# Routing rebuilt and traced first; two score blocks of the next quarter moved into the old one

## Chip, cores and metric

The kernel runs on one core of a Trainium2 chip. The metric is device time in microseconds, the median of several executions. TensorE (PE in the profile) multiplies matrices, VectorE (DVE), ScalarE (ACT) and GpSimd (POOL) work on elements, SyncE (SP) issues most transfers. SBUF is the on-chip memory, PSUM the accumulators that TensorE writes, in banks of 512 fp32 columns.

## Reference

Three parts, one after the other: an attention with random exponential features over 4 batches, 8 heads, 576 positions; a mixture of 8 experts in which each token takes the expert of its largest logit; and a dense network.

```python
q_p, k_p = (phi(q_s), phi(k_s))          # phi: exp(x @ omega.T - |x|^2/2 - row maximum)
kv = np.einsum('bhsm,bhsd->bhmd', k_p, v)
...
num = np.einsum('bhsm,bhmd->bhsd', q_p, kv)
den = np.einsum('bhsm,bhm->bhs', q_p, z)[..., None] + 1e-06
...
logits = x @ w_gate
expert_idx = np.argmax(logits, axis=1)
probs = np.exp(logits_shift)
probs /= probs.sum(-1, keepdims=True) + 1e-09
...
    h = np.maximum(xe @ w1[e], 0.0)
    ye = h @ w2[e]
    out[mask] = gate_w[mask, None] * ye
...
h = x @ w_in
g = h * (1.0 / (1.0 + np.exp(-1.702 * h)))
return (g @ w_out).astype(np.float32)
```

## The kernel before

The attention is worked in eight quarters, each half of a batch's heads (four heads). For each quarter `qgen` handles the queries and `kgen` the keys. `ph_P` is a score block: TensorE multiplies transposed queries or keys with omega into a PSUM tile `pr`, VectorE takes the row maximum (L359) into a slot of the one-bank PSUM tile `small`, two small operations (L368) combine it with half the squared norm, and a subtraction (L380) writes `qp` or `kp`. `X` transposes `qp` on TensorE and ScalarE takes the exponent into `qpT`; `N` multiplies it with `kv` and VectorE normalises (L446 to L455) into `xn`; `XT` (the R steps) transposes `xn` into the tile `tx` and, for the last 64 positions, into columns 0 to 63 of `small`, from where ScalarE writes the high part `xh` and VectorE the low part `xl`. `Q_ORDER` lists the order of these steps in a quarter; it has 17.

`route(b)` follows when both quarters of batch b are done. It multiplies `xh` and `xl` with the gate weights (`lT_ps`, two halves), copies the 16 rows (high and low part of the weights) to `lT`, transposes them, adds the halves, marks each token's largest logit (`oh`), counts the tokens of each expert with a product against ones (`ct_ps`), takes the index of the largest count (`ci`, `es`) and reads it into a register of SyncE. The expert weights w1[e], w2[e] of the batch are then requested in eight pieces by `pump` and `stage` (`st`), split into `wh` and `wl`, and multiplied by `moe_gen` (`m_ps`): the kernel works the expert that most tokens of a batch take, and tokens of another expert are handled by a loop at the end that is entered only if there are any. The products of a batch can't begin before its routing; batch 0's routing runs in the third quarter.

The order in which work is written down ("traced") is made by generators: `merge` always calls the part with the smallest share of its weight done (query steps weight 17, routing `ROUTE_N`, keys 5), and an outer loop alternates attention and experts by summed costs. A scheduler then orders each engine's queue, with earlier traced work first where it expects it to be ready. Each engine, and SyncE's transfer queue, works its queue in order.

```python
parts = [(qgen(i), W_Q)]
if pending is not None:
    parts.append((route(pending), ROUTE_N))
```

## Time and profile before

| | us |
|---|---|
| median of 3 runs | 767.72 (767.65 to 769.79) |
| the profiled execution | 767.65 |
| its span, first to last instruction | 765.6 |
| TensorE busy | 739.7 |
| VectorE busy | 531.3 |
| ScalarE busy | 338.6 |
| GpSimd busy | 131.9 |

The span is what the profile's rows add up to; the profiled execution's own time is 2.05 us longer and is what the prediction is made against. Busy shares are averages over stages with different limits, so the stages are read by themselves.

### The profile page before, as it was taken

What the parts mean: (1) busy time and instruction counts of PE and PEld (TensorE: products, weight loads), DVE (VectorE), ACT (ScalarE), POOL (GpSimd) and SP (SyncE); (2) the same over time, 40 slices, a digit from 0 to 9 for tenths busy, and PEclk for the clock granted to TensorE, in tenths of its full rate; (3) what the DMA queues carried; (4) which work ended last, traced back from release to release, by engine and by line L of the source; (5) the groups of instructions that cost most, each with busy time, mean ns of one, the idle gap of its engine ahead of it and who ended that gap; (6) DMA issues with size and microseconds to landing.
All of it is one profiled execution on the core that took longest, in us unless ns stands there. A gap on an engine that the chain in (4) does not pass through costs nothing.

```text
span 765.6 us, 14359 instructions
## 1 busy us (share of the span) xinstructions
PE 739.7 (97%) x5559; PEld 716.1 (94%) x5559; DVE 531.3 (69%) x1188; ACT 338.6 (44%) x638; POOL 131.9 (17%) x78
## 2 busy tenths in 40 slices
PE   7998799999999999989999999999999999999997
PEld 6877699999999999979999999999999999999996
DVE  5867867586776685556879559981368777777774
ACT  5554464335522332233427464554576433444331
POOL 3563377609500441000000000000000000000000
PEclk9999799999999999999999999999999999999999
DMA  5447594456725554198145558972978544443311
GB/s 157 117 131 187 123 302 97 120 140 193 189 60 162 150 179 134 51 234 287 59 161 197 177 171 295 316 263 100 332 273 298 172 138 138 137 129 117 115 29 32
DMA packets 136715, 127.57 MB, mean 167 GB/s; under 512 B 58176, under 2 KB 120896, under 8 KB 135744
## 3 DMA queue, kind: packets, MB, share of 16 engines
q1 hardware_dynamic: 123936, 98.85, 43.5%
q10 hardware_dynamic: 12704, 27.73, 10.3%
q8 instruction: 45, 0.74, 0.4%
q14 instruction: 30, 0.25, 0.1%
HBM read 79.68 MB, written 40.40 MB: 157 GB/s over the span
## 4 chain that ended last, share of the span: by engine, by line
PE 83%; DVE 8%; DMA 4%; issue 1%; ACT 1%; SPq 1%; POOL 0%; ACTq 0%; POOLq 0%; DVEq 0%
PE m_ps L136 19%; PE qa L1249 13%; PE qa L1146 13%; PE qm L1249 7%; PE w_ps L136 4%; PE pb L1249 3%; PE qm L1146 3%; PE qu L1146 3%; PE num L444 3%; PE kv_ps L402 3%; DMA st<-in_moe_w_dram 2%; PE qn L1146 2%; PE qt L1146 2%; PE tq L430 1%; PE pr L344 1%
## 5 line engine op out<-in xcount | busy, mean ns | idle before, releaser
L1146 PE MATMUL qa<-y,wi 128*128 128x384 f32 x576 | 109.2, 337 | 0.4 <-DVE g L901 0.4
L1146 PEld LDWEIGHTS qa<-y,wi 128*128 128x128 f32 x576 | 101.4, 188 | 0.8 <-DVE g L901 0.8
L136 PE MATMUL m_ps<-xh,wh 128*128 128x288 f32 x256 | 79.0, 309 | 4.1 <-DVE h1l L735 2.3
L136 PE MATMUL m_ps<-xh,wl 128*128 128x288 f32 x256 | 76.8, 300 | 0.1
L136 PE MATMUL m_ps<-xl,wh 128*128 128x288 f32 x256 | 76.4, 298 | 0.0
L700 POOL TENSOR_TENSOR wl<-st,wh 128x1024 fp32r<-128x1024 f32 x23 | 55.1, 2401 | 83.0 <-ACT wh L698 82.9
L359 DVE TENSOR_REDUCE small<-pr 128x4 f32<-128x512 f32 (+1 forms) x80 | 51.1, 639 | 11.8 <-PE pr L351 7.8
L698 ACT ACTIVATE wh<-st 128x1024 fp32r<-128x1024 f32 (+1 forms) x33 | 34.0, 1035 | 48.5 <-DMA st<-in_moe_w_dram 31.6
L136 PEld LDWEIGHTS m_ps<-xh,wh 128*128 128x128 f32 x256 | 48.6, 190 | 5.8 <-DVE h1l L735 3.6
L136 PE MATMUL m_ps<-h1h,wh 128*128 128x288 f32 x160 | 48.8, 305 | 0.9 <-DVE h1l L735 0.9
L136 PEld LDWEIGHTS m_ps<-xh,wl 128*128 128x128 f32 x256 | 48.6, 190 | 0.5 <-DVE wl L700 0.4
L735 DVE SCALAR_TENSOR_TENSOR h1l<-m_ps,h1h 128x288 fp32r<-128x288 f32 x64 | 28.9, 453 | 28.9 <-ACT h1h L732 28.8
L136 PEld LDWEIGHTS m_ps<-xl,wh 128*128 128x128 f32 x256 | 48.6, 190 | 0.0
L136 PE MATMUL m_ps<-h1l,wh 128*128 128x288 f32 x160 | 47.7, 298 | 0.0
L136 PE MATMUL m_ps<-h1h,wl 128*128 128x288 f32 x160 | 47.4, 298 | 0.0
L732 ACT ACTIVATE h1h<-m_ps 128x288 fp32r<-128x288 f32 x64 | 25.9, 407 | 48.5 <-PE m_ps L136 46.7
L1249 PE MATMUL qa<-p,p 128*128 128x256 f32 x360 | 46.2, 282 | 1.1 <-DVE p L855 0.8
L1249 PE MATMUL qa<-p,gs 128*128 128x256 f32 x360 | 45.9, 282 | 0.0
L1249 PEld LDWEIGHTS qa<-p,p 128*128 128x128 f32 x360 | 44.2, 189 | 1.6 <-DVE p L855 1.0
L1249 PEld LDWEIGHTS qa<-p,gs 128*128 128x128 f32 x360 | 44.2, 189 | 0.0
L444 PEld LDWEIGHTS num<-kv,qpT 128*128 128x128 f32 (+1 forms) x320 | 36.7, 184 | 5.4 <-ACT qpT L432 3.1
L444 PE MATMUL num<-kv,qpT 128*128 128x65 f32 (+1 forms) x320 | 39.3, 266 | 2.5 <-ACT qpT L432 1.4
(213 smaller groups left out, 1819.5 us busy)
## 6 DMA issues: line engine op xcount, KB each, us to landing
g_dram<-g ACTq DMA_DIRECT2D x48, 384.0 KB, 4.1
st<-in_moe_w_dram SPq DMA_DIRECT2D x31, 512.0 KB, 5.2
pg<-g_dram SPq DMA_DIRECT2D x10, 1024.0 KB, 5.7
raw<-in_moe_w_in_dram SPq DMA_DIRECT2D x16, 512.0 KB, 4.0
gt<-g_dram SPq DMA_DIRECT2D x8, 1024.0 KB, 5.4
p<-wo_dram SPq DMA_DIRECT2D x6, 1024.0 KB, 7.3
yt<-y_dram SPq DMA_DIRECT2D x12, 384.0 KB, 6.0
vm<-in_v_dram SPq DMA_DIRECT2D x32, 128.0 KB, 3.2
```

The costliest lines, as they stand in the source:

```text
L136: ins = nc.tensor.matmul(out=ps, lhsT=a, rhs=b, start=start and n == 0, stop=stop and n == 2)
L344: nc.tensor.matmul(out=ps[:, :, h2], lhsT=xT[:, (2 * pr + h2) * 2 + t0 // 2], rhs=wbd)
L359: nc.vector.tensor_reduce(out=pm, in_=ps[:, :w], axis=AX.X, op=ALU.max, negate=on_act)
L402: nc.tensor.matmul(out=kv_ps[:, h, :], lhsT=kp[j // 2][:, j % 2, h2, :], rhs=vm[:, h, t, :], start=(t == 0), stop=False,)
L430: nc.tensor.transpose(tq[:, c, h2], qp[i][:, c, h2, :], ident)
L444: nc.tensor.matmul(out=ps[:n, c, h2, :], lhsT=lhsT, rhs=kv[:, h, :])
L698: nc.scalar.activation(out=hi[:, :, s], in_=st[:, :, s], func=ACTF.Copy)
L700: eng.tensor_tensor(out=lo[:, :, s], in0=st[:, :, s], in1=f32(hi)[:, :, s], op=ALU.subtract)
L732: nc.scalar.activation(out=hh[:, f], in_=ps, func=ACTF.Relu)
L735: nc.vector.scalar_tensor_tensor(out=hl[:, f], in0=ps, scalar=0.0, in1=f32(hh[:, f]), op0=ALU.max, op1=ALU.subtract)
L1146: ins = nc.tensor.matmul(out=ps, lhsT=w[:, a, ks], rhs=y[:, b, kk], start=start and kk + m == 0, stop=kk == 1 and m == 2, skip_group_check ...
L1249: ins = nc.tensor.matmul(out=ps, lhsT=x[:, f], rhs=w[i][:, f], start=start and f + m == 0, stop=f == NP - 1 and m == 2, skip_group_check=True,
```

## The change

Routing gets the weight 40 in `merge`, in every quarter that has one. The logits' transposition becomes a product with a 16 by 8 matrix `fold` that adds the halves, into columns 256 to 295 of `small`; the counts go to columns 384 to 423 of `small`, with a product of their own for the last 64 positions in place of a cleared one-hot. The expert's number is read, and the weights requested, before exponent and gate are computed; the per-token index is made from the one-hot and `left` (8 minus the expert's number) instead of five searches for maximum and index. `F0` and `F1` in `Q_ORDER` compute score blocks 0 and 1 of the next quarter, which skips them.

```diff
--- before.py
+++ after.py
@@ -62,7 +62,7 @@
     XQ = nc.sync
     DVE_LO = 1
     KPRE = 6
-    ROUTE_N = 10
+    ROUTE_N = 40
     HP_ROUTE = 0
     HP_SPLIT = (0, 3)
     HP_STAGE = (0,)
@@ -72,7 +72,7 @@
     W_Q = 17
     W_K = 5
     K_ORDER = (0, 1, 4, 2, 3)
-    Q_ORDER = "P0 P1 X0 P4 X1 N0 P2 X4 N1 X2 P3 N4 X3 N2 R0 N3 R1"
+    Q_ORDER = "P0 P1 X0 P4 X1 N0 P2 X4 N1 X2 P3 N4 X3 N2 F0 R0 N3 F1 R1"
     LAG_E = 2
     LAG_X = 1
     LAG_M = 0
@@ -183,6 +183,7 @@
     QB = H // QH
     NQ = B * QB
     asked = []
+    first = {}
     clock = [0]
     late = []
 
@@ -420,7 +421,7 @@
         src, kv = q_in.pop(i), kv_t.pop(i)
         xn = att.tile([P, T + 1, QH, D], F32, tag="xn", name="xn", bufs=1)
         xv = xn.rearrange("p t h d -> p t (h d)")
-        qp, qt = {}, {}
+        qp, qt = first.pop(i, {}), {}
 
         def X(i):
             w = 2 if i < 4 else 1
@@ -485,7 +486,9 @@
                 xh_t[b] = (moe if b % 2 else xep).tile([P, KD, S], F32R, tag="xh", name="xh", bufs=1)
                 xl_t[b] = (moe if b % 2 else xep).tile([P, KD, S], F32R, tag="xl", name="xl", bufs=1)
             if op[0] == "P":
-                c = ph_P(i, src, qp, "qp", 3, g)
+                c = 0 if g in qp else ph_P(i, src, qp, "qp", 3, g)
+            elif op[0] == "F":
+                c = ph_P(i + 1, q_in[i + 1], first.setdefault(i + 1, {}), "qp", 3, g) if i + 1 < NQ else 0
             else:
                 c = {"X": X, "N": N, "R": XT}[op[0]](g)
             if n == 0 and i + 1 < NQ:
@@ -507,6 +510,12 @@
 
 
     gate_t, reg_t = {}, {}
+    lgx = att.tile([P, 2, E], F32, name="lgx")
+    fold, left = lgx[:2 * E, 0], lgx[:, 1]
+
+    def setup_route():
+        nc.vector.tensor_tensor(out=fold, in0=ident[:2 * E, 0:E], in1=ident[:2 * E, E:2 * E], op=ALU.add)
+        nc.vector.tensor_scalar(out=left, in0=iota8, scalar1=-1.0, scalar2=float(E), op0=ALU.mult, op1=ALU.add)
 
     def route(b):
         g = route_steps(b)
@@ -520,7 +529,8 @@
     def route_steps(b):
         yield 0
         xh, xl = xh_t[b], xl_t[b]
-        lT = att.tile([2 * E, S], F32, tag="dg", name="lT", bufs=1)
+        lT = att.tile([2 * E, (T + 1) * P], F32, tag="dg", name="lT", bufs=1)
+        nc.vector.memset(lT[:, S:], 0.0)
         for hf, tg in ((0, "n"), (1, "u")):
             c = slice(hf * HS, (hf + 1) * HS)
             lT_ps = pp.tile([2 * E, HS], F32, tag=tg, name="lT_ps", bufs=1)
@@ -531,36 +541,21 @@
             nc.scalar.activation(out=lT[:, c], in_=lT_ps, func=ACTF.Copy)
         yield 2.0
         yield 0
-        lg_ps = pp.tile([P, T + 1, 2, E], F32, tag="n", name="lg_ps", bufs=1)
+        lg_ps, ct_ps = (
+            small[:, x:x + (T + 1) * E].rearrange("p (t e) -> p t e", e=E) for x in (2 * P, 3 * P)
+        )
         for t in range(T + 1):
-            n = P if t < T else TAIL
-            nc.tensor.transpose(
-                lg_ps[:n, t].rearrange("p a e -> p (a e)"), lT[:, t * P:t * P + n], ident[:2 * E, :2 * E]
-            )
-        lg2 = att.tile([P, T + 1, 2, E], F32, tag="lg2", name="lg2", bufs=1)
-        nc.vector.memset(lg2[:, T], 0.0)
-        nc.vector.tensor_copy(lg2[:, 0:T], lg_ps[:, 0:T])
-        nc.vector.tensor_copy(lg2[:TAIL, T], lg_ps[:TAIL, T])
-        lg = att.tile([P, T + 1, E], F32, tag="lg", name="lg", bufs=1)
-        nc.vector.tensor_tensor(out=lg, in0=lg2[:, :, 0], in1=lg2[:, :, 1], op=ALU.add)
-
-
+            nc.tensor.matmul(out=lg_ps[:, t], lhsT=lT[:, t * P:(t + 1) * P], rhs=fold)
         rm = att.tile([P, T + 1, 1], F32, tag="rm", name="rm", bufs=2)
-        nc.vector.tensor_reduce(out=rm, in_=lg, axis=AX.X, op=ALU.max)
+        nc.vector.tensor_reduce(out=rm, in_=lg_ps, axis=AX.X, op=ALU.max)
         oh = att.tile([P, T + 1, E], F32, tag="oh", name="oh", bufs=2)
-        nc.vector.tensor_tensor(out=oh, in0=lg, in1=rm.to_broadcast([P, T + 1, E]), op=ALU.is_equal)
-        nc.vector.memset(oh[TAIL:, T, :], 0.0)
-        ex = att.tile([P, T + 1, E], F32, tag="ex", name="ex", bufs=2)
-        nc.vector.tensor_tensor(
-            out=ex, in0=lg, in1=rm.to_broadcast([P, T + 1, E]), op=ALU.subtract
-        )
-        nc.scalar.activation(out=ex, in_=ex, func=ACTF.Exp)
+        nc.vector.tensor_tensor(out=oh, in0=lg_ps, in1=rm.to_broadcast([P, T + 1, E]), op=ALU.is_equal)
         yield 0.5
         yield 0
-        ct_ps = pp.tile([P, T + 1, E], F32, tag="n", name="ct_ps", bufs=1)
         nc.tensor.matmul(
-            out=ct_ps.rearrange("p t e -> p (t e)"), lhsT=ones, rhs=oh.rearrange("p t e -> p (t e)")
+            out=ct_ps[:, 0:T].rearrange("p t e -> p (t e)"), lhsT=ones, rhs=oh[:, 0:T].rearrange("p t e -> p (t e)")
         )
+        nc.tensor.matmul(out=ct_ps[:, T], lhsT=ones[:TAIL, :], rhs=oh[:TAIL, T])
         ct = att.tile([P, E], F32, tag="ct", name="ct", bufs=2)
         nc.vector.tensor_reduce(out=ct, in_=ct_ps.rearrange("p t e -> p e t"), axis=AX.X, op=ALU.add)
         cm = att.tile([P, 8], F32, tag="cm", name="cm", bufs=2)
@@ -569,6 +564,16 @@
         nc.vector.max_index(ci, cm, ct)
         es = att.tile([P, 1], I32, tag="es", name="es", bufs=B)
         nc.vector.tensor_copy(es, ci[:, 0:1])
+        reg_t[b] = nc.values_load(
+            es[0:1, 0:1], engines=[mybir.EngineType.SP], min_val=0, max_val=E - 1,
+            skip_runtime_bounds_check_because="an index of the largest of E counts",
+        )
+        pump()
+        ex = att.tile([P, T + 1, E], F32, tag="ex", name="ex", bufs=2)
+        nc.vector.tensor_tensor(
+            out=ex, in0=lg_ps, in1=rm.to_broadcast([P, T + 1, E]), op=ALU.subtract
+        )
+        nc.scalar.activation(out=ex, in_=ex, func=ACTF.Exp)
         gate = att.tile([P, T + 1, 1], F32, tag="gate", name="gate", bufs=2)
         nc.vector.tensor_reduce(out=gate, in_=ex, axis=AX.X, op=ALU.add)
         nc.vector.tensor_scalar(out=gate, in0=gate, scalar1=1e-9, scalar2=None, op0=ALU.add)
@@ -582,13 +587,10 @@
                 )
         cif = att.tile([P, 1], F32, tag="cif", name="cif", bufs=2)
         nc.vector.tensor_copy(cif, ci[:, 0:1])
-        mx = att.tile([P, T + 1, 8], F32, tag="lmx", name="lmx", bufs=1)
-        ix = att.tile([P, T + 1, 8], U32, tag="lix", name="lix", bufs=1)
-        for t in range(T + 1):
-            nc.vector.max(mx[:, t], lg[:, t])
-            nc.vector.max_index(ix[:, t], mx[:, t], lg[:, t])
         ixf = att.tile([P, T + 1, 1], F32, tag="ixf", name="ixf", bufs=1)
-        nc.vector.tensor_copy(ixf, ix[:, :, 0:1])
+        nc.vector.tensor_tensor(out=oh, in0=oh, in1=left.unsqueeze(1).to_broadcast([P, T + 1, E]), op=ALU.mult)
+        nc.vector.tensor_reduce(out=ixf, in_=oh, axis=AX.X, op=ALU.max)
+        nc.vector.tensor_scalar(out=ixf, in0=ixf, scalar1=-1.0, scalar2=float(E), op0=ALU.mult, op1=ALU.add)
         eq = att.tile([P, T + 1, 1], F32, tag="eq", name="eq", bufs=1)
         nc.vector.tensor_scalar(out=eq, in0=ixf, scalar1=cif[:, 0:1], scalar2=None, op0=ALU.is_equal)
         nc.vector.memset(eq[TAIL:, T, :], 0.0)
@@ -601,11 +603,6 @@
         nc.vector.tensor_tensor(out=total, in0=total, in1=hit, op=ALU.subtract)
         nc.vector.tensor_copy(rr[:, :, 1:2], gate)
         yield 0.5
-        reg_t[b] = nc.values_load(
-            es[0:1, 0:1], engines=[mybir.EngineType.SP], min_val=0, max_val=E - 1,
-            skip_runtime_bounds_check_because="an index of the largest of E counts",
-        )
-        pump()
         nc.sync.dma_start(
             out=r_dram[b * S:b * S + T * P].rearrange("(p t) c -> p t c", t=T), in_=rr[:, 0:T]
         )
@@ -1007,6 +1004,7 @@
         halves_T(q_in, 0, nc.vector if DVE_LO else nc.gpsimd)
         load_qk(k, k_in, 1)
         setup_wg()
+        setup_route()
         halves_T(k_in, 1, nc.vector if DVE_LO else nc.gpsimd)
         A, Mg = attention_gen(), moe_all()
         done_a = done_m = 0.0
```

## Rows read from the trace of the kernel before

**Rows 1.** The page, part 1: busy time, share of the span, instructions of each engine.

```profile
PE 739.7 (97%) x5559; PEld 716.1 (94%) x5559; DVE 531.3 (69%) x1188; ACT 338.6 (44%) x638; POOL 131.9 (17%) x78
```

**Rows 2.** Busy time in stretches of 20 us: length, engines, PEclk, DMA share, GB/s.

```profile
100.00:120.00 20.00, 20.00 (x176) 19.61 (x175) 14.25 (x39) 13.60 (x22) 16.89 (x9) 1.00 0.72 209
...
320.00:340.00 20.00, 18.20 (x132) 17.32 (x132) 12.17 (x35) 7.98 (x16) 0.00 (x0) 1.00 0.82 211
```

**Rows 3.** The same in stretches of 5 us, columns as in rows 2.

```profile
45.00:50.00 5.00, 3.54 (x22) 2.55 (x21) 4.36 (x11) 2.09 (x7) 4.84 (x3) 1.00 0.84 222
50.00:55.00 5.00, 5.00 (x24) 4.20 (x22) 3.55 (x14) 2.92 (x8) 3.86 (x3) 0.66 0.01 2
75.00:80.00 5.00, 3.54 (x39) 3.01 (x40) 4.61 (x19) 4.28 (x12) 4.40 (x3) 1.00 0.01 2
80.00:85.00 5.00, 3.88 (x29) 3.35 (x29) 4.92 (x33) 1.15 (x4) 2.58 (x2) 0.66 0.44 102
85.00:90.00 5.00, 3.62 (x32) 3.11 (x33) 4.91 (x25) 1.56 (x5) 0.00 (x0) 0.78 0.61 137
90.00:95.00 5.00, 3.16 (x23) 2.61 (x22) 2.01 (x7) 2.10 (x8) 0.00 (x0) 0.84 0.76 188
95.00:100.00 5.00, 4.98 (x33) 4.83 (x34) 2.86 (x9) 4.37 (x10) 2.33 (x1) 0.70 1.05 363
```

**Rows 4.** Chain of waits, 86 to 96 us: start, length, what.

```profile
89.22 4.37 DMA st<-in_moe_w_dram
```

**Rows 5.** Timeline of all engines, 72 to 96 us: start, length, engine, line, operation.

```profile
73.41 0.69 ACT L531 ACTIVATE lT<-lT_ps 16x288 f32<-16x288 f32 x2 [2.42 <-PE lT_ps L530]
...
76.63 2.38 POOL L308 TENSOR_TENSOR hl<-m,hl 128x1152 f16<-128x1152 f32 x1 [0.52 <-DVE small L359]
...
78.18 0.45 PE L537 MATMUL lg_ps<-ident,lT 16*128 16x16 f32 x5
...
79.90 1.35 DVE L545 TENSOR_TENSOR lg<-lg 128x40 f32<-128x40 f32 x1
...
82.01 5.73 SPq L309 DMA_TRANSPOSE xT<-hl  x2
...
82.39 0.33 DVE L551 TENSOR_TENSOR oh<-lg,rm 128x40 f32<-128x40 f32 x1
...
84.98 0.39 PE L561 MATMUL ct_ps<-oh,ones 128*128 128x40 f32 x2 [0.76 <-DVE xn L455]
...
86.27 0.16 DVE L569 FIND_INDEX8 ci<-cm,ct 128x8 uint32<-128x8 f32 x1
...
88.26 0.15 DVE L571 CAST es<-ci 128x1 int32<-128x1 uint32 x1
...
89.22 5.97 SPq L674 DMA_DIRECT2D st<-in_moe_w_dram  x8
...
94.30 0.40 PE L136 MATMUL m_ps<-xh,wh 128*128 128x288 f32 x1 [1.73 <-ACT wh L698]
```

**Rows 6.** Groups of VectorE instructions from 71.4 to 89.2 us.

```profile
L359 DVE TENSOR_REDUCE small<-pr 128x4 f32<-128x512 f32 (+1 forms) x9 | 5.7, 634 | 0.2
...
L549 DVE TENSOR_REDUCE rm<-lg 128x5 f32<-128x40 f32 x1 | 0.2, 197 | 0.0
```

**Rows 7.** Timeline of all engines, 66 to 72 us, where the second quarter ends.

```profile
67.00 0.27 PE L466 MATMUL small<-ident,xn 64*128 64x64 f32 x1
...
67.77 0.22 PE L351 MATMUL pr<-wl,xT 128*128 128x128 f16 x1
...
68.83 1.17 ACT L307 ACTIVATE hl<-m 128x1152 f16<-128x1152 f32 x1 [2.84 <-DMA m<-in_k_dram]
...
70.14 0.23 DVE L473 TENSOR_TENSOR xl<-small,xh 128x64 fp32r<-128x64 f32 x1 [4.40 <-ACT xh L469]
...
71.48 0.70 DVE L359 TENSOR_REDUCE small<-pr 128x4 f32<-128x512 f32 x1
```

**Rows 8.** Timeline of all engines, 38 to 50 us, where the first quarter ends.

```profile
45.07 0.23 DVE L473 TENSOR_TENSOR xl<-small,xh 128x64 fp32r<-128x64 f32 x1 [3.36 <-ACT xh L469]
```

## Prediction

> **What bounds the kernel now.** I read the page first: TensorE is busy 739.7 us of a span of 765.6 [rows 1], so over the whole span it is the bound, and only its idle time, its low clock and added products can move the end. Then the busy times in stretches: from 100 us on TensorE is busy 20.00 us of 20, while VectorE has room [rows 2]; time won by VectorE alone is worth nothing there. What can be won lies before 100 us, where the experts' products have not begun. The 5 us stretches [rows 3] show it: TensorE idles 1.46 us (75 to 80), 1.12, 1.38 and 1.84 us (90 to 95), and the granted clock falls to between 0.66 and 0.84 from 80 to 100 us. A mean of 0.66 means that part of the stretch ran at 1.2 GHz instead of 2.4; the products lost are about busy time times (1 minus clock): 1.3, 0.8, 0.5 and 1.5 us from 80 on.
>
> The chain of waits says what ends that stretch: the transfer of the first expert weights, asked for at 89.22 and 4.37 us long [rows 4], after which the first expert product runs at 94.30 [rows 5]. The transfer needs the expert's number, and the timeline [rows 5] shows how late it is. The logits lie in SBUF at 74.10 (73.41 + 0.69); their transposition runs at 78.18, the sum of halves from 79.90 for 1.35 us, the one-hot at 82.39, the count at 84.98 (held by VectorE's xn, because its PSUM bank is shared), the index is found at 86.27 and cast at 88.26: 14.2 us for a few small operations. The groups of VectorE from 71.4 to 89.2 say why: score blocks stand between them, nine maximum reductions alone taking 5.7 us, with 0.2 us of idle [rows 6]. VectorE's order, not the operations' cost, sets the request.
>
> **The routing.** With a weight of 40 its seven steps take 7/40 = 0.175 of the merge, under three query steps of 17 (0.176); with 10 they reached to 0.70, twelve query steps. So only one key block and one query step's work stay between them. I rebuild the chain from rows, starting at 74.10. Fp32 products of two operands show as two instructions each (the one count call of rows 5 is x2), a transposition as one (x5 for five calls); so five logit calls become ten instructions, at 0.45/5 each: 0.90, to 75.00. The maximum 0.20 [rows 6] and the one-hot 0.33 [rows 5] follow directly, without memset, two copies and sum: 75.53. From the count's start to the end of the index search is 1.45 us (84.98 to 86.43), and the second count call adds 0.39 [rows 5]: 77.37. From the cast's start to the request is 0.96 (88.26 to 89.22): 78.33. Landing 4.37 later and a product 0.71 after that (94.30 less 93.59) give 83.4. Lower bound: that, with no other work between. Upper bound: a score chain, about 1.3 us (12 us of score work over nine, estimated from rows 6: reduction 0.63, two small sums, subtraction), at each of three hand-overs: 87.4. I take half a chain, 84.0, since first-traced work goes first where it is ready: 10.3 us earlier.
>
> Worth: from 84.0 the idle time that the experts' products can fill is 0.2 + 1.38 + 1.84 = 3.4, and the low clock from 85 on, 0.8 + 0.5 + 1.5 = 2.8 [rows 3]; the drop of 80 to 85 I leave standing. Against it, the score work that VectorE did between 71.5 and 84 now comes later, so TensorE has less to do before the weights land: nothing at best, 3.4 at worst (all that was won). I take the middle, 1.7.
>
> SyncE's queue: the request is moved ahead of the two crossbar transposes that stand at 82.01 [rows 5]. Their source is only finished by GpSimd at 79.01 (76.63 + 2.38), so a request at 78.3 meets a free queue; behind it eight requests hold SyncE for 5.97 us, to 84.3, and the later transposes slip by some 2 us. They feed the quarter after next, and expert products cover that; if they did not, 2 us would be lost. The register read waits on the index with only those transposes and the r_dram stores queued behind.
>
> **Products.** Five further logit passes (0.45) and two count passes (0.39) are 0.84 us per routing at most, nothing at least if they fall into other gaps; I take 0.5. Three routings lie where TensorE is full: 1.5 us lost. In the first it is inside the 84.0. The set-up of the two constants and the zeroed logit tail are one or two small VectorE operations in places where TensorE does not wait for them; the 15 index-search instructions per routing that go, and the exponent that now follows the request, are VectorE time off the path. Without the cover of full TensorE they would be a gain, so I count nothing.
>
> **The two early score blocks.** They add no work; they fill a hole. At the end of the second quarter, score products are done by 68.0, yet VectorE idles 4.40 us for ScalarE's copy, which sits behind a conversion that waited 2.84 us for a key load; the next reduction starts at 71.48 [rows 7]. The first boundary has the same hole, 3.36 us before 45.07 [rows 8]. An early block goes into it, so the next quarter's first transposition need not wait for the reduction after the copies. At the first boundary TensorE idles 1.46 us (45 to 50) and runs at 0.66 from 50 to 55, some 1.7 us [rows 3]: 3.2 at most, nothing at least if the second block only delays the second tail transposition. I take half, 1.6. At the second boundary the gain is already in the 84.0. Later boundaries lie under a full TensorE: nothing; if uncovered, again up to 1.6 each.
>
> **Sum.** 3.4 + 2.8 - 1.7 + 1.6 - 1.5 = 4.6 us less. The profiled execution took 767.65 us for a span of 765.6; the median shown is 767.72, practically the same. Forecast: 763.0.
>
> **A rule that speaks against it.** In rows 7 no VectorE operation touches `small` between 67.0, where the first tail transposition writes it, and the copy at 70.14, though scores are ready; at 71.48 the reduction starts as soon as the last copy is done. So users of that bank seem to take turns in traced order, and now the logits and counts join them.
> The Trainium skill, PSUM — Partial Sum Buffer, section PSUM bank collisions raise a hardware error, wants engines kept apart by whole bank, not by address, and its summary says to read a different bank from the one products go to. The trace agrees, with the 71.48. By this rule the sum would be that of the slower rival below, 770.7; by the hole alone 763.0.
>
> **Rivals.**
> Slower: the shared bank. All score blocks traced after the routing wait until the count is written, so VectorE stands still from about 71.5 to 75.0 waiting for logits, 3.5 us in a stretch where it had no gap; the second early block puts its reduction and sums (about 1.0) ahead of the second tail transposition and so ahead of the logits; the added products cost 1.5: 6.0. If by these the expert products start only at 91, what is left to win is 1.5 idle and 1.5 clock, and the time is 767.65 + 3.0 = 770.7. It decides from a start later than about 87.5, where cost and gain meet. For it: the turns in rows 7. Against: VectorE has other work then (square sums, normalisations), and the rebuilt chain is short.
> No change: the request does not move. If SyncE's order keeps the transposes ahead of the register read, the request waits until 87.74 (82.01 + 5.73), 1.5 us earlier than now: 0.7 won, plus 1.6, less 1.5: 766.9. For it: the queue works in order. Against: the transposes' source is later than my index.
> More than forecast: everything above at its good bound, and the routing of the last quarter also frees the 1.80 us idle of 320 to 340 [rows 2]: 3.4 + 2.8 + 3.2 + 1.8 = 11.2, that is 756.5.
>
> **Chances.** Measured differences below 0.3%, 2.3 us, can't be told from none. The forecast with its spread to the good side 0.68 (its own range 757.0 to 765.3), no change 0.19, slower 0.13. Eight in ten from 757.0, near the good bound, to 769.0, into the slower rival. Faster 0.68, same 0.19, slower 0.13.
>
> **What would show it.** Right: es cast near 77 and the weight request near 79; first expert product near 84; full clock from 90 on; VectorE without a hole at 42 to 45; busy TensorE in 100 to 280 unchanged. Wrong: the request behind the transposes; a VectorE hole between the last copy and the count; new TensorE idle after 100 us, above all at 320 to 360, where the end of attention meets the last experts.

## The result, and the profile after

The changed kernel took 776.25 us (median of 4 runs, 772.24 to 779.82), the kernel before 767.68 beside it: ratio 1.0103, 95% interval 1.0069 to 1.0136. It is slower by 1%; 763.0 was forecast, and 776.25 lies outside the range of 757 to 769. The profiled execution took 777.14 us for a span of 775.2; all rows of the changed kernel below are from it. Medians and ratios here and below leave out five executions of 1030 to 4058 us, two of them of the kernel before, which were in a slower state.

The page, part 1, of the changed kernel, beside [rows 1]: TensorE is busy 6.1 us longer with 28 instructions more, VectorE 13.3 us less. VectorE's saving bought nothing.

```profile
PE 745.8 (96%) x5587; PEld 723.3 (93%) x5587; DVE 518.0 (67%) x1122; ACT 337.4 (44%) x638; POOL 132.0 (17%) x78
```

The start of the experts came nearly as forecast. Timeline of the changed kernel, 72 to 86 us, beside [rows 5]:

```profile
72.23 0.40 ACT L541 ACTIVATE lT<-lT_ps 16x288 f32<-16x288 f32 x1 [0.65 <-PE lT_ps L540]
...
73.27 1.28 PE L548 MATMUL small<-lgx,lT 16*128 16x8 f32 x10
...
74.58 0.20 DVE L550 TENSOR_REDUCE rm<-small 128x5 f32<-128x40 f32 x1 [1.54 <-PE small L548]
...
76.65 0.58 PE L555 MATMUL small<-oh,ones 128*128 128x32 f32 x2
...
77.15 0.59 PE L558 MATMUL small<-oh,ones 64*128 64x8 f32 x2
...
77.78 0.20 DVE L560 TENSOR_REDUCE ct<-small 128x8 f32<-128x40 f32 x1 [2.76 <-PE small L558]
...
80.80 0.14 DVE L566 CAST es<-ci 128x1 int32<-128x1 uint32 x1
...
81.66 4.19 SPq L671 DMA_DIRECT2D st<-in_moe_w_dram  x6
...
85.11 0.59 PE L136 MATMUL m_ps<-xh,wh 128*128 128x288 f32 x1
```

The request goes out at 81.66 instead of 89.22, the first expert product runs at 85.11 instead of 94.30. But look at the brackets: VectorE stands idle 1.54 us for the logits and 2.76 us for the counts, where the nine reductions of [rows 6] had 0.2 us of idle before them. And ten logit passes take 1.28 us where five transpositions took 0.45. The stretches of 5 us (columns as in [rows 2]), beside [rows 3]:

```profile
45.00:50.00 5.00, 4.21 (x27) 3.22 (x25) 4.62 (x17) 2.52 (x8) 4.84 (x3) 1.00 0.79 220
50.00:55.00 5.00, 4.38 (x28) 3.50 (x28) 3.62 (x12) 2.95 (x7) 3.68 (x3) 1.00 0.00 0
...
65.00:70.00 5.00, 3.38 (x34) 2.83 (x34) 1.63 (x4) 2.15 (x5) 2.24 (x1) 1.00 0.90 251
70.00:75.00 5.00, 4.06 (x34) 3.01 (x32) 2.55 (x9) 2.31 (x6) 3.80 (x4) 0.99 0.50 129
75.00:80.00 5.00, 4.16 (x24) 4.07 (x24) 2.24 (x9) 2.11 (x7) 4.84 (x3) 0.50 0.00 0
80.00:85.00 5.00, 2.99 (x16) 2.46 (x15) 4.16 (x24) 1.24 (x4) 0.85 (x1) 0.50 0.42 115
85.00:90.00 5.00, 5.00 (x32) 4.85 (x32) 4.17 (x13) 2.82 (x7) 0.82 (x1) 0.64 1.00 314
90.00:95.00 5.00, 5.00 (x51) 4.51 (x50) 3.71 (x12) 4.22 (x9) 5.00 (x3) 1.00 1.06 386
```

From 90 us on TensorE is full at full clock, as forecast. Ahead of it stand ten microseconds at 1.2 GHz (0.50), which were not; they follow on ten in which TensorE was busy 3.38 and 4.06 of 5. And 100 us further on there are holes where the kernel before had 20.00 of 20. Stretches of 20 us, first of the kernel before, then of the changed kernel:

```profile
160.00:180.00 20.00, 20.00 (x178) 19.00 (x176) 13.13 (x60) 8.03 (x17) 6.64 (x3) 1.00 0.73 195
180.00:200.00 20.00, 20.00 (x191) 19.45 (x190) 16.37 (x49) 10.97 (x19) 18.82 (x10) 1.00 0.77 209
...
260.00:280.00 20.00, 20.00 (x163) 19.68 (x162) 16.46 (x31) 6.40 (x13) 8.22 (x4) 1.00 0.58 175
```

```profile
160.00:180.00 20.00, 16.69 (x158) 15.73 (x156) 15.78 (x58) 6.72 (x13) 5.67 (x3) 1.00 0.87 185
180.00:200.00 20.00, 19.98 (x166) 19.21 (x167) 11.12 (x33) 10.72 (x18) 13.61 (x7) 0.91 0.87 234
...
260.00:280.00 20.00, 18.24 (x148) 17.39 (x147) 15.21 (x33) 5.34 (x11) 5.09 (x3) 1.00 0.75 233
```

**An account of the span.** I cut each profiled span into stretches of 4 us, the last one ending with the span, and added up TensorE's idle time (4 less busy) and the time lost to a low clock (busy times 1 minus granted clock). What is left of the span is TensorE's work at full clock. Before: lost 20.9 up to 100 us, 3.9 from 100 to 400, 7.1 after, together 32.0 with rounding; work 733.6. After: 18.3, 12.1, 7.9, together 38.4; work 736.8. So of the 9.6 us of span, 3.2 are work, and 6.4 are lost time: 2.6 won at the front, 8.2 lost in the middle, 0.8 lost at the end.

### The profile page after: what moved, and what is told of

Read it like the earlier page. It is cut to its first block, busy times and chain, and to the rows that moved or that the text cites. A ratio compares the mean times of both kernels' runs of the same rounds, so it can differ in the third digit from the quotient of the medians.

```text
span 775.2 us, 14359 instructions
## 1 busy us (share of the span) xinstructions
PE 745.8 (96%) x5587; PEld 723.3 (93%) x5587; DVE 518.0 (67%) x1122; ACT 337.4 (44%) x638; POOL 132.0 (17%) x78
## 4 chain that ended last, share of the span: by engine, by line
PE 53%; DVE 1%; DMA 1%; issue 0%; ACT 0%; DVEq 0%; ACTq 0%
PE qa L1247 13%; PE qa L1144 13%; PE qm L1247 7%; PE m_ps L136 5%; PE pb L1247 3%; PE qm L1144 3%; PE qu L1144 3%; PE w_ps L136 3%; PE qn L1144 2%; PE qt L1144 1%; DMA st<-in_moe_w_dram 1%; DVE p L852 0%; DVE wl L697 0%; ACT wh L695 0%; DVE ob L1260 0%
```

## The experiments

All kernels compute the whole result, with parts of the change switched on or off or done in another way. I had three theories. Q, queues: with the request early, the later weight pieces and the crossbar transpositions stand in each other's way on SyncE, and ScalarE, which works in order, waits for a late piece. B, bank: users of the PSUM bank `small` take turns, and the routing now joins them. P, products: the extra TensorE passes cost more than the 1.5 us forecast. From the second group on there is a fourth, O: any change of the order moves the waits further on, whichever edit makes it. Times and accounts of all kernels, in us; ratios are to the kernel before, run on the same chip (766.5 to 766.8 us there); "lost" is the account above, up to 100 us / 100 to 400 / after 400:

| kernel | median | ratio, 95% | profiled span | lost | work |
|---|---|---|---|---|---|
| only_early_blocks | 765.66 | 1.0001 [0.9980, 1.0022] | 763.7 | 17.8 / 7.8 / 6.9 | 731.2 |
| only_traced_first | 764.77 | 0.9967 [0.9944, 0.9989] | 763.0 | 17.7 / 7.3 / 6.9 | 731.1 |
| only_rebuilt | 780.00 | 1.0175 [1.0153, 1.0196] | 777.4 | 22.3 / 9.8 / 6.9 | 738.4 |
| first_in_batch0 | 770.29 | 1.0048 [1.0031, 1.0064] | 767.9 | 18.4 / 5.4 / 6.9 | 737.2 |
| rebuilt_own_bank | 773.05 | 1.0069 [1.0043, 1.0095] | 772.0 | 18.2 / 9.2 / 6.8 | 737.7 |
| rebuilt_transposed | 781.81 | 1.0186 [1.0164, 1.0209] | 780.4 | 23.3 / 14.7 / 6.9 | 735.5 |
| first_and_early | 767.26 | 1.0013 [0.9991, 1.0034] | 764.0 | 16.7 / 7.9 / 6.8 | 732.6 |
| after_own_transposed | 774.42 | 1.0102 [1.0081, 1.0122] | 772.6 | 17.4 / 14.0 / 6.9 | 734.4 |
| request_late | 775.05 | 1.0098 [1.0064, 1.0132] | none read | | |
| only_early_request | 765.99 | 0.9999 [0.9979, 1.0019] | 763.7 | 19.6 / 4.5 / 6.9 | 732.7 |
| only_first_batch0 | 769.33 | 1.0037 [1.0023, 1.0051] | 774.2 | 20.0 / 15.1 / 6.8 | 732.3 |
| first_early_batch0 | 771.86 | 1.0077 [1.0054, 1.0099] | 770.7 | 16.0 / 15.9 / 7.2 | 731.7 |
| first_early_index | 769.27 | 1.0033 [1.0016, 1.0049] | 768.2 | 23.0 / 5.3 / 6.9 | 733.1 |
| first_early_count | 763.54 | 0.9956 [0.9940, 0.9972] | 762.7 | 14.8 / 7.9 / 6.9 | 733.1 |
| after_stage_first | 771.86 | 1.0087 [1.0056, 1.0118] | 768.8 | 17.7 / 8.1 / 6.9 | 736.1 |
| traced_stage_first | 763.87 | 0.9964 [0.9942, 0.9987] | 765.2 | 18.1 / 9.3 / 6.9 | 730.9 |
| after_wh_pool | 771.60 | 1.0069 [1.0042, 1.0097] | 768.9 | 16.9 / 7.7 / 6.9 | 737.4 |
| traced_wh_pool | 765.51 | 0.9987 [0.9968, 1.0006] | 764.2 | 20.9 / 6.8 / 6.9 | 729.6 |

The windows round to 0.01, so the work column is good to some two microseconds. A profiled execution can also stand several microseconds from its kernel's median (774.2 of span, 776.41 us, for only_first_batch0 with a median of 769.33). Each account is of one execution, so a difference of a few us between two accounts can also be one between two executions.

**The three parts, one at a time.** The early blocks alone:

```diff
-    Q_ORDER = "P0 P1 X0 P4 X1 N0 P2 X4 N1 X2 P3 N4 X3 N2 R0 N3 R1"
+    Q_ORDER = "P0 P1 X0 P4 X1 N0 P2 X4 N1 X2 P3 N4 X3 N2 F0 R0 N3 F1 R1"
```

> The kernel before with the two early score blocks alone. Theory Q (queues: in the changed kernel ScalarE's queue stood 8.56 us before a weight split whose transfer was late, between 169 and 178 us, because routing is traced first also in later batches) gives these blocks no part in the loss: 765 to 768. Theory B (bank: everything that uses the tile small takes turns) adds about 1 us per uncovered boundary: 768 to 771, with a hole of VectorE between the copy of the tail and the next reduction. Theory P (products: 28 more product instructions, 3.2 us) gives no change: 766 to 768.

Routing traced first alone:

```diff
-    ROUTE_N = 10
+    ROUTE_N = 40
```

> The kernel before with the routing weight 40 alone. Theory Q: the weight pieces of batch 1 come before other work in ScalarE's queue, so the stall at 160 to 200 us appears here too (some 3 to 5 us), against a gain before 100 us of 2 to 4: 766 to 772. Theories B and P have their cause in the rebuilt routing, which is not in this kernel, so the gain before 100 us stands alone: 762 to 766, and TensorE is busy 20.00 of 20 from 160 to 200.

The rebuilt routing alone, that is the changed kernel with both of the above undone:

```diff
-    ROUTE_N = 40
+    ROUTE_N = 10
...
-                c = 0 if g in qp else ph_P(i, src, qp, "qp", 3, g)
+                c = ph_P(i, src, qp, "qp", 3, g)
```

> The kernel before with the rebuilt routing alone, weight 10 as before and no early blocks. Theory Q: no stall at 160 to 200; products cost some 3 us, the shorter chain gives back 1 to 2: 767 to 770. Theory B: score blocks between logits and counts make both wait, the request of the first weights comes later than the 89.2 us of before: 771 or more. Theory P alone: 769 to 771.

The changed kernel with routing first in batch 0 only:

```diff
-                parts.append((route(pending), ROUTE_N))
+                parts.append((route(pending), ROUTE_N if pending == 0 else 10))
```

> The changed kernel with weight 40 for the routing of batch 0 only, 10 for batches 1 and 2. Theory Q: the stall of 5.0 us (idle 3.3 and low clock 1.7) at 160 to 200 us goes, that at 260 to 280 perhaps too: 768 to 772. Theories B and P: the same holes and the same products, 774 to 778.

Early blocks alone change nothing, routing first alone wins 0.3%, and the rebuilt routing alone loses 13 us (780.0 against 766.6): it is the part that costs, and more than P or Q said. first_in_batch0 came inside Q's band, and its interval lies below the whole change's. Timeline of only_rebuilt, 80 to 93 us:

```profile
80.21 1.28 PE L545 MATMUL small<-lgx,lT 16*128 16x8 f32 x10
...
81.53 0.20 DVE L547 TENSOR_REDUCE rm<-small 128x5 f32<-128x40 f32 x1 [1.73 <-PE small L545]
...
82.37 2.76 SPq L309 DMA_TRANSPOSE xT<-hl  x1
...
86.54 0.59 PE L555 MATMUL small<-oh,ones 64*128 64x8 f32 x2
...
87.17 0.20 DVE L557 TENSOR_REDUCE ct<-small 128x8 f32<-128x40 f32 x1 [1.50 <-PE small L555]
...
89.93 0.14 DVE L563 CAST es<-ci 128x1 int32<-128x1 uint32 x1
...
92.26 1.01 SPq L668 DMA_DIRECT2D st<-in_moe_w_dram  x2
```

The two holes are B's. The request goes out at 92.26, 3 us later than before the change, though fewer operations lead to it: the cast is 1.7 us later, and 1.4 us more lie between the cast and the request (2.33 against 0.96). The holes are the slower rival's mechanism, here without routing first and without early blocks.

**Bank against products.** The rebuilt routing with logits and counts in their old bank (the exponent moved ahead of the count again), then the rebuilt routing with the old one-pass transpositions:

```diff
-        lg_ps, ct_ps = (
-            small[:, x:x + (T + 1) * E].rearrange("p (t e) -> p t e", e=E) for x in (2 * P, 3 * P)
-        )
+        lg_ps = pp.tile([P, T + 1, E], F32, tag="n", name="lg_ps", bufs=1)
...
+        ct_ps = pp.tile([P, T + 1, E], F32, tag="n", name="ct_ps", bufs=1)
```

> The rebuilt routing alone (weight 10, no early score blocks), but with logits and counts in the PSUM bank that the old routing used (tag n) instead of the shared bank small; since that bank then turns from the logits to the counts, the exponent's subtraction stands ahead of the count again. Theory B (the bank small taken in turns is what the rebuild costs): the VectorE holes of 1.73 and 1.50 us behind the logits and the counts go, the request comes back to 89 to 90, and the time falls from 780.0 to 770 to 774. Theory P (the added products cost it): the rebuilt logits stay ten passes of 1.28 us, the counts four; the time stays at 777 to 781. Theory O (the planner's order of the following work, changed by the different set of operations, costs it, not any one of them): the time moves by a few us to either side, and the losses stand in other stretches.

```diff
-            nc.tensor.matmul(out=lg_ps[:, t], lhsT=lT[:, t * P:(t + 1) * P], rhs=fold)
+            nc.tensor.transpose(
+                lg2_ps[:, t].rearrange("p a e -> p (a e)"), lT[:, t * P:(t + 1) * P], ident[:2 * E, :2 * E]
+            )
+        nc.vector.tensor_copy(lg2, lg2_ps)
+        nc.vector.tensor_tensor(out=lg_ps, in0=lg2[:, :, 0], in1=lg2[:, :, 1], op=ALU.add)
```

> The rebuilt routing alone, in the shared bank small, but the logits come by the one-pass transposition of both halves, one copy and one sum on VectorE, as before, instead of fp32 products that sum in PSUM: five TensorE instructions of about 0.09 us instead of ten of 0.13, two VectorE operations more. Theory P (added products): about 1.28 less 0.45 in each of four routings, 2 to 3.5 us less: 776 to 778. Theory B (bank turns): the turns stay, with a copy more in the chain: 779 to 782. Theory O: a few us to either side, with other stretches losing.

Timeline of rebuilt_own_bank, 79 to 88 us:

```profile
79.32 1.28 PE L543 MATMUL lg_ps<-lgx,lT 16*128 16x8 f32 x10
...
81.86 0.19 DVE L545 TENSOR_REDUCE rm<-lg_ps 128x5 f32<-128x40 f32 x1
...
86.62 0.19 DVE L561 TENSOR_REDUCE ct<-ct_ps 128x8 f32<-128x40 f32 x1
```

The brackets are gone, VectorE does other work until it comes to the maximum, the request comes back to 89.08, and 7 us of the 13 go with the holes: B holds in this setting. The exponent's place was moved along with the bank and was not tried by itself. The remaining 6 us are near P's 5. rebuilt_transposed came out inside B's band (779 to 782), not P's. But its account says that P's term exists too: its work falls to 735.5, 2.9 less than only_rebuilt, and the lost time grows by 5.9 and hides it. The groups of TensorE instructions price the term directly; first the kernel before, then the changed kernel (output, input, shapes, count; busy time in all, mean ns of one):

```profile
L537 PE MATMUL lg_ps<-ident,lT 16*128 16x16 f32 (+1 forms) x20 | 2.0, 208 | 0.0
...
L561 PE MATMUL ct_ps<-oh,ones 128*128 128x40 f32 x8 | 1.4, 255 | 0.8 <-DVE xn L455 0.8
```

```profile
L548 PE MATMUL small<-lgx,lT 16*128 16x8 f32 x40 | 5.3, 254 | 0.0
...
L558 PE MATMUL small<-oh,ones 64*128 64x8 f32 x8 | 1.8, 289 | 0.0
L555 PE MATMUL small<-oh,ones 128*128 128x32 f32 x8 | 1.5, 278 | 0.0
```

5.3 + 1.8 + 1.5 less 2.0 and 1.4 is 5.2 us in four routings. The accounts agree: the six kernels with the whole rebuild's products stand at 736.1 to 738.4 (mean 737.3), the ten with neither of its products, the kernel before among them, at 729.6 to 733.6 (mean 731.9). The groups do not overlap, and their means are 5.4 apart.

**The change without the rebuild, and the whole change without bank and products.**

```diff
-    ROUTE_N = 10
+    ROUTE_N = 40
...
-    Q_ORDER = "P0 P1 X0 P4 X1 N0 P2 X4 N1 X2 P3 N4 X3 N2 R0 N3 R1"
+    Q_ORDER = "P0 P1 X0 P4 X1 N0 P2 X4 N1 X2 P3 N4 X3 N2 F0 R0 N3 F1 R1"
```

> The old routing, traced first in all quarters, and the two early score blocks: the change without the rebuilt routing. If the rebuild alone is what makes the change slower (theories B and P), 762 to 766, that of routing first alone (764.8) or a little better. If routing first and early blocks do harm together (theory Q: late weight pieces in SyncE's queue, stall of ScalarE at 160 to 200), 768 to 772.

after_own_transposed is the changed kernel with the two edits of the pair above.

> The whole change, but with logits and counts in their old PSUM bank (tag n) and the logits by the one-pass transposition, a copy and a sum; of the rebuild only the one-hot index, the split count and the early request remain. B and P together: near routing first with early blocks, 762 to 767. If the early request or the index (theory Q again, the queue's order) is the cost: 771 to 776.

The first came to 767.3, between its two bands and not to be told from the kernel before. The second came to 774.4: the whole change with its bank turns and its extra logit passes taken away is as slow as the whole change (1.0102 against 1.0103). Its work fell by 2.4 us, and its lost time stayed (38.2 for 38.4). So in the whole change B and P are not the sum of the matter; the band of the early request or the index, 771 to 776, was hit, and the next runs take these two alone.

**The request, and batch 0 alone.** The request moved back in the changed kernel (the diff), and forward in the kernel before (the reverse of it):

```diff
         nc.vector.tensor_copy(es, ci[:, 0:1])
-        reg_t[b] = nc.values_load(
...
-        pump()
...
         yield 0.5
+        reg_t[b] = nc.values_load(
...
+        pump()
```

> The whole change, but the read of the expert's number and the weight requests stand behind the gate again, as before the change. What stays open after the first eight runs: with logits and counts in their old bank and the old transposition, the change still takes 7 us more than routing first with early blocks alone (774.4 against 767.3), and the edits left between them are the early request, the one-hot index and the split count. Theory Q (the early request, put ahead of the crossbar transposes in SyncE's queue, makes those late): 769 to 773 in place of 776. Theory N (the order of requests is not it; bank turns and added products are): 776 to 779, a little worse because the weights are asked for later.

> The kernel before, in which only the read of the expert's number and the weight requests are moved ahead of the gate and the index operations. By the prediction's reading of SyncE's queue the first request moves from 89.2 to at most 88.7, so nothing is won: 765 to 768. Theory Q (requests ahead of transposes cost in the later batches): 769 to 773. Theory N: no change within 2 us.

The kernel before with the weight of 40 in batch 0 only, without and with early blocks:

```diff
-                parts.append((route(pending), ROUTE_N))
+                parts.append((route(pending), 40 if pending == 0 else ROUTE_N))
```

> The kernel before, with routing traced first (weight 40) only for batch 0. With all four first it was 764.8; its trace lost 5.2 us at 160 to 200, where ScalarE stood for batch 1's third weight piece. Theory Q (routing first does harm in the later batches, where TensorE is full): 760 to 763. If the later batches' order is not the cause: 764 to 766.

> The kernel before, with routing traced first only for batch 0 and the two early score blocks. If the early blocks are worth their 1.6 us at the first boundary when nothing else gets in the way: 758 to 761.5. If they only move waits (766.7 alone, against 766.7 before): the time of the kernel with batch 0 first alone, within 1.5 us.

The request's place is worth nothing that these runs could tell, either way: request_late lies in neither of its bands, and its interval overlaps the whole change's (of request_late no profile is read). And the last two, which lie above all of their bands, refute Q's reading, for the old routing, that routing first does harm in the later batches: batch 0 alone is worse (769.3, 771.9) than every batch (764.8, 767.3). In the rebuilt setting it was the other way round (first_in_batch0 770.3 against 776.3). The same edit helped in one setting and hurt in the other.

**The rest of the rebuild, and the stall at 160 to 200.** To first_and_early is added the index from the one-hot, or the count in two products:

```diff
-        for t in range(T + 1):
-            nc.vector.max(mx[:, t], lg[:, t])
-            nc.vector.max_index(ix[:, t], mx[:, t], lg[:, t])
+        nc.vector.tensor_tensor(out=oh, in0=oh, in1=left.unsqueeze(1).to_broadcast([P, T + 1, E]), op=ALU.mult)
+        nc.vector.tensor_reduce(out=ixf, in_=oh, axis=AX.X, op=ALU.max)
```

> Routing first with early blocks and the old routing (767.3), with one part of the rebuild added: the token's expert number from the one-hot (a product with E minus index, a maximum, one more small operation) in place of ten searches on VectorE. No product of TensorE is added. Theory P and B (added products and bank turns are the cost): 766 to 768.5. Theory I (the index operations stand where VectorE is needed, and their cost in lost time is what remains of the 7 us): 771 to 775. Theory O (any change of the order moves the losses): anywhere from 762 to 772.

```diff
-        nc.vector.memset(oh[TAIL:, T, :], 0.0)
-            out=ct_ps.rearrange("p t e -> p (t e)"), lhsT=ones, rhs=oh.rearrange("p t e -> p (t e)")
+            out=ct_ps[:, 0:T].rearrange("p t e -> p (t e)"), lhsT=ones, rhs=oh[:, 0:T].rearrange("p t e -> p (t e)")
+        nc.tensor.matmul(out=ct_ps[:, T], lhsT=ones[:TAIL, :], rhs=oh[:TAIL, T])
```

> Routing first with early blocks and the old routing (767.3), with the other part added: the count in two products, the second over the tail's tokens alone, and no clearing of the tail's one-hot. TensorE does two passes more in each of four routings, by the rows 2.9 us of counting instead of 1.6. Theory P: 768 to 769.5. Theory O: anywhere from 762 to 772; if it comes to 773 or more, the second count is the cost by a way I don't see.

The index costs 2 us, with intervals that overlap; the two products win 4, with intervals that do not, though they add passes: 763.5, 0.4% under the kernel before. Neither is the missing 7 us, and their sum has the wrong sign; O is what is left, by elimination and not by a run that shows it.

The stall that is largest in the changed kernel's middle is at 175 to 180. Its timeline:

```profile
167.23 4.81 SPq L310 DMA_TRANSPOSE xT<-hl  x1
...
172.34 0.40 SPq L671 DMA_DIRECT2D st<-in_moe_w_dram  x1
...
177.91 1.06 ACT L695 ACTIVATE wh<-st 128x1024 fp32r<-128x1024 f32 x1 [8.56 <-DMA st<-in_moe_w_dram]
...
180.02 0.66 PE L465 MATMUL tx<-ident,xn 128*128 128x128 f32 x4 [3.33 <-ACT qpT L433]
```

Batch 1's third weight piece is asked for behind a transposition; ScalarE stands 8.56 us for it, the copy of qpT stands behind that, and TensorE behind the copy. Two tries at this chain, each in the changed kernel and in only_traced_first:

```diff
-    HP_STAGE = (0,)
+    HP_STAGE = (0, 1, 2, 3)
```

> The whole change, with the weight requests of all four batches given the priority that only batch 0's have now, so that they stand ahead of the crossbar transposes in SyncE's queue where their buffer is free. Theory S (the loss at 160 to 200 comes from ScalarE standing 8.56 us for a weight piece that was asked for behind a transposition of 4.81 us): that wait shrinks to under 5 us, the 5.0 us lost at 160 to 200 go, and the time is 770 to 773. Rival: the buffer itself is late (two of them, each freed only when its piece is converted), and the time stays at 775 to 778.

> Routing first alone (764.8), with the weight requests of all four batches given batch 0's priority. It lost 5.2 us at 160 to 200 in its own profile, with the same wait of TensorE for ScalarE's copy as the whole change. Theory S: 759.5 to 762.5. Rival (the buffer is late): 764 to 767.

```diff
+                if b == 1 and c in (2, 3):
+                    nc.gpsimd.tensor_copy(hi[:, :, s], st[:, :, s])
+                else:
                     nc.scalar.activation(out=hi[:, :, s], in_=st[:, :, s], func=ACTF.Copy)
```

> The whole change, with the first conversion of batch 1's third and fourth weight pieces done by GpSimd instead of ScalarE, so that GpSimd and not ScalarE stands for the late piece. Theory W (at 160 to 200 TensorE starves because ScalarE, standing 8.56 us for the piece, can't copy out qpT): TensorE's wait for qpT there goes, the 5.0 us lost at 160 to 200 fall below 2.5, and the time is 771 to 773.5. Rival (the loss moves elsewhere, as it did with the earlier edits of the order): 160 to 200 is mended, and the time stays at 774.5 to 778. If 160 to 200 still loses 4 us or more, ScalarE's stand was not its cause.

> Routing first alone (764.8), with the first conversion of batch 1's third and fourth weight pieces done by GpSimd instead of ScalarE. Theory W: the 5.2 us lost at 160 to 200 fall below 2.5, and the time is 760.5 to 762.5, below every kernel so far. Rival (the loss moves elsewhere): 763.5 to 766.

The priority did not do what it was to do: in after_stage_first the request still followed a transposition (170.73 behind 166.12 + 4.31), ScalarE still stood 8.1 us, and 160 to 200 still lost 5.8 us (5.4 in traced_stage_first, whose 763.9 lies in neither of its bands). That 771.9 lies in the band of theory S is luck: its interval overlaps the whole change's, and what its profile lost less was at 240 to 360. The queue's order was not tested by it. With GpSimd standing in ScalarE's place the stall is mended, and another takes its place. Stretches of 5 us of after_wh_pool, and the wait that ends the second hole:

```profile
175.00:180.00 5.00, 5.00 (x45) 4.76 (x44) 3.44 (x11) 2.14 (x5) 3.19 (x2) 1.00 1.16 304
...
190.00:195.00 5.00, 2.17 (x19) 1.82 (x16) 3.27 (x10) 3.03 (x5) 4.21 (x2) 1.00 0.96 241
195.00:200.00 5.00, 4.59 (x31) 4.44 (x31) 3.51 (x12) 3.18 (x6) 5.00 (x4) 0.70 0.56 144
```

```profile
195.41 0.65 PE L431 MATMUL tq<-ident,qp 128*128 128x128 f32 x4 [2.86 <-ACT qpT L433]
```

175 to 180 is full, where the changed kernel has 1.69 of 5, and 190 to 195 has 2.17, where it has 5.00. From 160 to 200 the kernel still loses 4.7 us (the changed kernel 5.0), and traced_wh_pool 5.2. ScalarE's stand ends the wait that the profile names, but it is not what the loss hangs on: 771.6 lies in the band of theory W without W's mechanism, and traced_wh_pool came out in the rival's. Next I looked at the busy time of the expert products (m_ps) alone: of the kernel before, of the changed kernel, and of first_early_count:

```profile
185.00:190.00 5.00, 0.90 (x7) 0.92 (x8) 0.00 (x0) 0.00 (x0) 1.00 0.83 216
```

```profile
175.00:180.00 5.00, 1.04 (x6) 0.83 (x6) 0.00 (x0) 0.00 (x0) 1.00 1.21 335
190.00:195.00 5.00, 0.00 (x0) 0.00 (x0) 0.00 (x0) 0.00 (x0) 1.00 0.73 165
```

```profile
185.00:190.00 5.00, 0.88 (x5) 0.70 (x6) 0.82 (x2) 0.57 (x2) 1.00 0.66 197
```

In the kernel before they have a gap at 185 to 190, and TensorE stays full through it; in the changed kernel at 175 to 180 and 190 to 195. A tempting reading is that the first gap is the hand-over from batch 0's products to batch 1's: started 9 us earlier, they run out 10 us earlier, and the attention work that filled the gap before is not ready ten microseconds sooner. The runs speak against it. In first_early_count the first product runs at 83.78, earlier still, and the gap stays at 185 to 190; TensorE, here with all its work, is full:

```profile
160.00:180.00 20.00, 20.00 (x181) 19.24 (x180) 10.66 (x34) 9.88 (x16) 9.55 (x5) 1.00 0.97 250
180.00:200.00 20.00, 20.00 (x188) 19.40 (x188) 17.02 (x52) 10.69 (x22) 20.00 (x10) 1.00 0.78 210
```

And rebuilt_transposed, whose first product runs at 98.4, later than before the change, loses 6.2 us from 160 to 200. So an early start is neither enough for this loss nor needed for it, and its cause stays open.

## Why the prediction was wrong, point by point

**The start: right in its time, in part by luck.** First product at 85.11 for 84.0, inside the bounds of 83.4 and 87.4, and the request stood ahead of the transpositions. But the request came at 81.66 for 78.3, and from there to the product it took 3.45 us where the sum had 5.08 (4.37 and 0.71); one miss hid most of the other. And the rebuild was not what brought the early start: with the old routing the first product runs at 86.1 by routing first alone, and at 85.1 with the early blocks added.

**The front's worth: the term for the score work was too small.** 3.4 + 2.8 - 1.7 + 1.6 = 6.1 was forecast, 2.6 measured. From 84 to 100 the lost time fell from 7.1 to 2.3, by 4.8; from 40 to 60, where the early blocks were to bring 1.6, from 3.2 to 1.7, by 1.5. But from 60 to 84 it rose from 4.9 to 8.7: 3.9, where I had put 1.7 for "TensorE has less to do before the weights land", with 3.4 as the worst. The two holes of VectorE (1.54 and 2.76) lie in that stretch, and so do nine of the ten microseconds at 1.2 GHz. But the holes are not what it hangs on: only_traced_first, with the old routing in its old bank, loses 9.1 there, at a low clock too, and first_and_early 8.2. Stretches of only_traced_first:

```profile
70.00:75.00 5.00, 2.78 (x24) 1.81 (x21) 4.07 (x14) 2.94 (x7) 4.66 (x4) 1.00 0.34 79
75.00:80.00 5.00, 2.17 (x14) 1.97 (x15) 4.92 (x28) 0.66 (x3) 4.84 (x3) 0.59 0.00 0
```

So the term was of the right kind, and too small. The single edit priced the bank at 7 us with the rebuilt routing alone; in the whole change no run has the bank alone undone.

**A rule on the bank.** With the shared bank VectorE stands idle until the logits and the counts are written (1.73 and 1.50 us in only_rebuilt); with a bank of their own the same two reductions show no wait, because score blocks, which write other addresses of `small`, run in between. The Trainium skill, PSUM — Partial Sum Buffer, section PSUM bank collisions raise a hardware error, wants engines kept apart by bank and not by address; the trace agrees, with these idle times. Whether the turns are kept for the bank or for `small` as one tile, which fills it, no run separates. The slower rival had this mechanism, and wanted a start later than 87.5 for it. The start was 85.1, so it was right about the holes, and wrong about the late start.

**Products: the term was mis-sized.** "0.84 us per routing at most", 0.5 taken, three routings: 1.5. Measured by the rows: 1.3 in each of four, 5.2; by the accounts of two executions 3.2, by the means of the two groups 5.4. I had priced a pass by the transposition's 0.09; it takes 0.128 (ten in 1.28 at full clock), and the second count call as much as the first.

**The cover from 100 us on: the step that failed.** The prediction counted what lies after 100 us at nothing because TensorE is full there [rows 2]: "later boundaries lie under a full TensorE: nothing", "expert products cover that". The changed kernel loses 8.2 us more from 100 to 400: 5.0 at 160 to 200, 2.1 at 240 to 360 and 1.1 in the rest. [rows 2] itself has 18.20 beside the 20.00, and the kernel before loses 3.9 us in all there. Full was a state of that order of work, not a reserve. TensorE idle after 100 us was one of the prediction's own signs of being wrong, though not at 160 to 200. None of the 17 profiled variants keeps the 3.9 us of before; they lose 4.5 to 15.9, whether their experts start earlier or later. Three kernels with the old routing that win at the front (early blocks 3.1, routing first 3.2, both 4.2 us) lose 3.9, 3.4 and 4.0 us more from 100 to 400, about as much as they won; first_early_count wins 6.1 and loses 4.0 more.

**The sum.** Forecast 6.1 won and 1.5 lost. Measured 2.6 won at the front, 8.2 lost in the middle, 0.8 lost at the end, 3.2 of work (5.2 by the rows, which is within the account's two microseconds): 9.6 us more span.

**What stays open.** Which edit makes the 8.2, and by what. Request, index and count, one at a time, are worth 0, +2 and -4 us, while the same three with the rebuilt transposition are worth +7 (after_own_transposed against first_and_early): the parts do not add. Ten kernels with the old logits, most of which differ in order alone, stand between 763.5 and 771.9. A third landing buffer for weight pieces, and transpositions on another queue than SyncE's, were not tried.

## What to carry to other kernels

A stretch in which the bounding engine is full is no proof of slack: a new order can open holes in it. Here every variant lost more from 100 to 400 us than the kernel before, those that started the experts earlier and those that started them later. Price a small fp32 product from a row of such a product and not from a transposition, and multiply by all its calls. Before moving a result into a bank that other work cycles through, count the users that would wait for their turn.

Of all kernels run, three are faster than the kernel before, by 0.3 to 0.4%: routing first (764.8), the same with all weight requests in priority (763.9), and routing first with early blocks and the count in two products (763.5).

## What the runs showed of the hardware

The weight load of an fp32 product with K = 16 (K is the length of the sum) took as long as one with K = 128: in the changed kernel the loads for the logits (16 x 128) have a median of 187 ns, those for the counts (128 x 128) 190. So a contraction of 16 made the load no shorter. The Trainium skill, TensorE: Matmul & The Clock Gate, section LDWEIGHTS (loading the stationary operand), says that the load goes by columns and not by the contraction; the rows agree.

The same kind of VectorE operation on 128 x 40 took 0.19 us (the exponent's subtraction at 77.90, one operand from PSUM) and 1.44 us (the one-hot's product at 78.00, both from SBUF) one behind the other. In the changed kernel, beside the GpSimd operation of that time:

```profile
77.28 2.11 POOL L268 TENSOR_TENSOR m<-m 128x1152 f32<-128x1152 f32 x1
...
78.00 1.44 DVE L591 TENSOR_TENSOR oh<-oh,lgx 128x40 f32<-128x40 f32 x1
```

GpSimd's operation ends at 79.39, VectorE's at 79.44. In three other kernels the same product began inside that same GpSimd operation, and ended 0.05 to 0.06 us after it: first_in_batch0 (79.83 behind 79.77), after_own_transposed (78.66 behind 78.61) and after_stage_first (78.25 behind 78.19). In rebuilt_own_bank it began at 86.73, with GpSimd idle since 83.81, and took 0.19. So in these runs the product of two SBUF operands stood until GpSimd's operation was done, and the subtraction with a PSUM operand did not. In the changed kernel the index search follows at 79.37, so by an estimate 1.25 us of the late request (1.44 less 0.19) is this.
